# Transposing a gating matrix once, during the first attention layer, instead of in each gating layer

## The chip, the cores and the metric

The kernel runs on one core of a Trainium2 chip, in one launch. The time is that of the device for one execution, in microseconds; five executions were timed, and one more was profiled. The engines are TensorE (PE, matmuls and transposes; PEld is its weight loading), VectorE (DVE), ScalarE (ACT), GpSimd (POOL) and SyncE (SP, which here issues all the transfers).

## The reference

The input x has 2048 rows of 512 numbers in bf16. Four layers follow one another, each added to x: attention, gating, attention, gating. Both attention layers have the same weights, and so have both gating layers.

```python
def _A_ref(x, wq, wk, wv, wo):          # 32 heads of 16, one shared k and v
    q = (x @ wq).reshape(B, S, H, Dh).transpose(0, 2, 1, 3)
    k = x @ wk
    v = x @ wv
    p = softmax(einsum('bhqd,bkd->bhqk', q, k) * Dh ** -0.5)
    o = einsum('bhqk,bkd->bhqd', p, v)
    return o.transpose(0, 2, 1, 3).reshape(B, S, H * Dh) @ wo

def _B_ref(x, w_in, w_sp, b_sp, w_out): # F = 1792, Fh = 896
    z = gelu(einsum('bsd,df->bsf', x, w_in))
    z1 = z[..., :Fh]
    z2 = layernorm(z[..., Fh:])
    g = einsum('ts,bsf->btf', w_sp, z2) + b_sp[None, :, None]
    return einsum('bsf,fd->bsd', z1 * g, w_out)

x = x + _A_ref(layernorm(x), ...)
x = x + _B_ref(layernorm(x), ...)
x = x + _A_ref(layernorm(x), ...)
x = x + _B_ref(layernorm(x), ...)
```

w_sp is a matrix of 2048 x 2048 that mixes rows of x. TensorE sums over the partition dimension, so the product with w_sp needs w_sp with its columns (s) in the partitions: its transpose.

## The kernel before

Every engine has one program, a list of operations in the order in which the Python code calls `K.op`; each operation waits for semaphore values and may raise a semaphore. So the order of the code is the order on each engine. Tiles have 128 partitions; x stays in SBUF as X for the whole kernel.

**Attention (`layer_A`).** After a layer norm (`layer_norm_T`: statistics, normalising, transposing by TensorE) come k, v and two of the 32 projections of q. Then a loop over i runs 683 times. The work is counted in blocks of 128 keys x 512 queries for one head; four heads make a unit (qc, hg, kt), of which there are 4 x 8 x 16 = 512. An iteration handles three blocks:

- `emit_exp(i)` (L585): ScalarE takes the exponential of three PSUM banks of scores at once, 128 x 1536.
- `emit_pv(u)` and `emit_acc(u)` (L600, L618, L620, L622) for a unit whose four blocks are done: TensorE multiplies with v, and VectorE adds the result to an accumulator. Unit u is done in iteration (4u+3)//3, so three of four iterations have a unit. L622 is the last unit of a group of 16, of which there are 32.
- `emit_fill(i + 2)` (L566): TensorE computes the three score blocks of the iteration after the next.
- One side task: `emit_side_pe` and `emit_side_dve` take the next of `side_queue`. The queue begins with the 30 remaining projections of q (L397, L402). Each finished group adds a final task, which transposes and divides by the softmax sum (L479, L484, L489); the last group of a query chunk adds two tasks that transpose (L511, L519) and four that multiply with wo and add to X (L529, L534). All side tasks share PSUM bank 7. What is in the queue when the loop ends is emitted behind it.

**Gating (`layer_B`).** After a layer norm, 60 items (32 of z2, 28 of z1) go through a software pipeline of five steps: matmuls (L695 or L700), square on ScalarE (L732), a multiply on VectorE (L741), tanh on ScalarE (L752), and a last multiply on VectorE (L762), for z2 with statistics (L767, L770). Each item uses one of six slots (PSUM bank, `ybuf`, `thbuf`); matmuls of item k wait for L762 of item k - 6. The five steps are emitted with lags of 0 to 4 items. ScalarE then normalises z2 (L795).

The second half goes through four blocks of 512 rows (tc). For each block, SP loads four times 128 rows of w_sp (L824, 512 KB) into `wsp_stage`, which has two slots; TensorE transposes them in groups of eight 128 x 128 pieces (L839), and VectorE copies each group from PSUM to `wspT` (L847). Then come 7 x 16 matmuls with `wspT` (L868), VectorE's add and multiply (L875, L881), four times seven matmuls with w_out (L897), and the add to X (L903). At the end SP stores X in 16 transfers (L918).

Of the kernel before, what the change touches and what calls it, by code (L numbers as in the profile page):

```python
# [6 lines left out]
BF16 = mybir.dt.bfloat16  # L7
# [97 lines left out]
def bass_interleave_layers__grouped_kv_mqa__mixer_gmlp__prompt_kernel(  # L105
# [13 lines left out]
    S = A_x.shape[1]  # L119
    assert A_x.shape[2] == D  # L120
    assert S % 128 == 0
    NT = S // 128
# [4 lines left out]
    TCW = QC  # L127
# [7 lines left out]
    S_wA = K.sem()  # L135
    S_wB = K.sem()
    S_wsp = [K.sem(), K.sem()]
    S_dpool = K.sem()
    S_pool = K.sem()
    S_ploc = K.sem()  # L140
# [19 lines left out]
    def bank16(b):  # L160
        return ps16[:, 1024 * b:1024 * (b + 1)]
# [77 lines left out]
        w_prep = (S_dve, w_prep_v)  # L239

    x_ready = [(S_x, S_x.n)]
    G = {"stage_free": [None, None]}

    def layer_norm_T(lst, x_waits, extra_pe_waits):
        xnT = K.sb([P, KD, S], BF16, lst, name="xnT")
# [51 lines left out]
        xst.__exit__(None, None, None)  # L297
        return xn, xnT, xnT_v

    def layer_A(layer_idx, x_waits):  # L300
        lst = ExitStack()
        lst.__enter__()
        xn, xnT, xnT_v = layer_norm_T(lst, x_waits, extra_pe_waits=[])
        xnT_all = (S_dve, max(xnT_v))
        qT_pad = K.sb([P, 8, S], BF16, lst, name="qT_pad")
# [121 lines left out]
            return (4 * u + 3) // 3  # L427

        side_queue = []
        side_state = {"k_pe": 0, "k_dve": 0}  # L430
        fin_pe_val = [None, None]
        x_done_vals = []

        def emit_side_pe():
            if side_state["k_pe"] >= len(side_queue):
                return False
            k = side_state["k_pe"]
            task = side_queue[k]
            if task.get("pe_ready") is not None and not task["pe_ready"]():
                return False  # L440
            wl = list(task["pe_waits"]) + [(S_sdve, sdve_base + k)]
            v = K.op("pe", task["pe"], waits=wl, inc=S_spe)
            task["pe_val"] = v
            if "on_pe_emitted" in task:
                task["on_pe_emitted"](v)
            side_state["k_pe"] += 1
            return True

        def emit_side_dve():
            if side_state["k_dve"] >= side_state["k_pe"]:  # L450
                return False
            k = side_state["k_dve"]
            task = side_queue[k]
            wl = list(task["dve_waits"]) + [(S_spe, task["pe_val"])]
            fns = task["dve"]
            v = None
            for idx, fn in enumerate(fns):
                wlx = wl if idx == 0 else [(S_dloc, v)]
                if idx < len(fns) - 1:
                    v = K.op("dve", fn, waits=wlx, inc=S_dloc)  # L460
                else:
                    v = K.op("dve", fn, waits=wlx, inc=S_sdve)
            task["dve_val"] = v
            if "on_dve_emitted" in task:
                task["on_dve_emitted"](v)
            side_state["k_dve"] += 1
            return True
# [3 lines left out]
        pv_bank = bank32(6)  # L471
        for (qc, hg) in q_groups[NQ_PRO:]:
            side_queue.append(make_q_task(qc, hg))

        def make_fin_task(qc, hg, par, acc_val):
            def pe_fn(e):
# [163 lines left out]
        for i in range(NI):  # L640
            emit_exp(i)
            for u in pending_pv.get(i, []):
                emit_pv(u)
                emit_acc(u)
            if i + 2 < NI:
                emit_fill(i + 2)
            emit_side_pe()
            emit_side_dve()
        for i in range(NI, NI + 8):
            for u in pending_pv.get(i, []):  # L650
                emit_pv(u)
# [1 line left out]
        while side_state["k_dve"] < len(side_queue) or side_state["k_pe"] < len(side_queue):  # L653
            progressed = emit_side_pe()
            progressed = emit_side_dve() or progressed
            if not progressed:
                break
        assert side_state["k_dve"] == len(side_queue)
        lst.__exit__(None, None, None)
        return [(S_sdve, max(x_done_vals))]  # L660

    def layer_B(layer_idx, x_waits):
        lst = ExitStack()
# [2 lines left out]
        xnT_all = (S_dve, max(xnT_v))  # L666
        z2n = K.sb([P, NT, FH], BF16, lst, name="z2n")
        z1c = K.sb([P, NF1, S], BF16, lst, name="z1c")
        NSLOT = 6
        ybuf = K.sb([P, NSLOT, 512], FP32, lst, name="ybuf")  # L670
        thbuf = K.sb([P, NSLOT, 512], BF16, lst, name="thbuf")
        st2 = K.sb([P, NT, 2, 6], FP32, lst, name="st2")
# [41 lines left out]
        def step_pe(k):  # L714
            it = items[k]
            slot = k % NSLOT
            bk = bank32(slot)
            wl = [xnT_all, wB]
            if k >= NSLOT:
                wl.append((S_dve, st["d4"][k - NSLOT]))  # L720
            st["pe"][k] = K.op("pe", lambda e, it=it, bk=bk: pe_item(e, it, bk), waits=wl, inc=S_pe)

        def step_a0(k):
            it = items[k]
            slot = k % NSLOT
            bk = bank32(slot)
            n = item_N(it)
            wl = [(S_pe, st["pe"][k])]
            if k >= NSLOT:
                wl.append((S_dve, st["d3"][k - NSLOT]))  # L730
                wl.append((S_act, st["a1"][k - NSLOT]))
            st["a0"][k] = K.op("act", lambda e, slot=slot, bk=bk, n=n: e.activation(  # L732
                ybuf[:, slot, 0:n], bk[:, 0:n], ACTF.Square, scale=SQA), waits=wl, inc=S_act)
# [38 lines left out]
        LAG = [0, 1, 2, 3, 4]  # L772
        for it_k in range(NIT + 5):
            k = it_k
            if k - LAG[0] < NIT and k - LAG[0] >= 0:
                step_pe(k - LAG[0])
            if 0 <= k - LAG[1] < NIT:
                step_a0(k - LAG[1])
            if 0 <= k - LAG[2] < NIT:
                step_d3(k - LAG[2])  # L780
            if 0 <= k - LAG[3] < NIT:
                step_a1(k - LAG[3])
            if 0 <= k - LAG[4] < NIT:
                step_d4(k - LAG[4])
        gelu_done = (S_dve, st["d4"][NIT - 1])
        z1_ready = gelu_done

# [9 lines left out]
                            waits=[(S_dve, vnb), gelu_done], inc=S_act)  # L797
        z2n_all = (S_act, vz2n[NT - 1])

        wsp_stage = K.sb([P, 2, S], BF16, lst, name="wsp_stage")  # L800
        wspT = K.sb([P, NT, TCW], BF16, lst, name="wspT")
        hT2 = K.sb([P, NF1, TCW], BF16, lst, name="hT2")
        gtmp = K.sb([P, 3, TCW], FP32, lst, name="gtmp")

# [2 lines left out]
        wt_bank_free = [None, None]  # L807
        g_bank_free = [None, None, None]
        y_bank_free = [None, None]
        wspT_free = None  # L810
        hT2_free = None
        x_vals = []
        gi_ctr = [0]
        ngrp = 8 if NT >= 8 else NT

        for tc in range(NTC):
            wspT_v = None
            for tt in range(NTT):
                trow = tc * NTT + tt
                slot = tt % 2  # L820
                wl = list(x_waits)
                if stage_free[slot] is not None:
                    wl.append((S_pe, stage_free[slot]))
                vdma_v = K.op("sp", lambda e, slot=slot, trow=trow: e.dma_start(  # L824
                    wsp_stage[:, slot, :], B_w_sp[trow * 128:(trow + 1) * 128, :]), waits=wl, inc=S_wsp[slot], incv=16)
                vdma = (S_wsp[slot], vdma_v)
                for g0 in range(0, NT, ngrp):
                    gsz = min(ngrp, NT - g0)
                    b = gi_ctr[0] % 2
                    bk = bank16(b)  # L830
                    wl = [vdma, (S_pool, v_ident), gelu_done]
                    if wt_bank_free[b] is not None:
                        wl.append((S_dve, wt_bank_free[b]))

                    def pe_tr(e, slot=slot, g0=g0, gsz=gsz, bk=bk):
                        ins = None
                        for k in range(gsz):
                            sti = g0 + k
                            ins = e.transpose(bk[:, k * 128:(k + 1) * 128], wsp_stage[:, slot, sti * 128:(sti + 1) * 128], ident[:])  # L839
                        return ins  # L840
                    vtr = K.op("pe", pe_tr, waits=wl, inc=S_pe)
                    stage_free[slot] = vtr

                    def dve_cp(e, g0=g0, gsz=gsz, tt=tt, bk=bk):
                        dst = wspT[:, g0:g0 + gsz, tt * 128:(tt + 1) * 128]
                        src = bk[:, 0:gsz * 128].rearrange("p (k q) -> p k q", q=128)
                        return e.tensor_copy(dst, src)  # L847
                    wlc = [(S_pe, vtr)]
                    if g0 == 0 and tt == 0 and wspT_free is not None:
                        wlc.append((S_pe, wspT_free))  # L850
                    vcp = K.op("dve", dve_cp, waits=wlc, inc=S_dve)
                    wt_bank_free[b] = vcp
                    wspT_v = vcp
                    gi_ctr[0] += 1
            wspT_ready = (S_dve, wspT_v)

            vh = [None] * NF1
            for ft in range(NF1):
# [3 lines left out]
                if g_bank_free[gb] is not None:  # L862
                    wl.append((S_dve, g_bank_free[gb]))

                def pe_g(e, ft=ft, bk=bk):
                    ins = None
                    for sti in range(NT):
                        ins = e.matmul(bk[:, 0:TCW], z2n[:, sti, ft * 128:(ft + 1) * 128], wspT[:, sti, :],  # L868
                                       start=(sti == 0), stop=(sti == NT - 1))
                    return ins  # L870
                vg = K.op("pe", pe_g, waits=wl, inc=S_pe)
                if ft == NF1 - 1:
                    wspT_free = vg
                wl = [(S_pe, vg), v_bsp_w]
                v1 = K.op("dve", lambda e, gb=gb, bk=bk, tc=tc: e.tensor_tensor(  # L875
                    gtmp[:, gb, :], bk[:, 0:TCW], bsp_bc[:, tc * TCW:(tc + 1) * TCW], ALU.add),
# [31 lines left out]
        return [(S_dve, max(x_vals))]  # L908

    xw = x_ready  # L910
    xw = layer_A(0, xw)
    xw = layer_B(1, xw)
    xw = layer_A(2, xw)
    xw = layer_B(3, xw)
# [2 lines left out]
    for t in range(NT):  # L917
        v = K.op("sp", lambda e, t=t: e.dma_start(out[0, t * 128:(t + 1) * 128, :], X[:, t, :]),  # L918
                 waits=list(xw), inc=S_out, incv=16)
    K.op("sp", lambda e: e.nop(nofuse=True), waits=[(S_out, v)])  # L920
    K.op("pool", lambda e: e.nop(nofuse=True), waits=[(S_out, v)])
    K.emit()


# [26 lines left out]
```

## Time and profile before

| what | value |
|---|---|
| median of five runs | 2753.64 us (2751.88 to 2755.23) |
| profiled execution | 2760.63 us, its span 2758.8 us |
| busy share of the span | PE 72%, PEld 20%, DVE 45%, ACT 76%, POOL 0% |
| mean granted TensorE clock | 0.627 of full speed |
| first attention layer, from its layer norm | about 23 to 1082 us of the span |
| first gating layer | about 1082 to 1387 us |
| second attention layer | about 1387 to 2447 us |
| second gating layer | about 2447 to 2756 us |

The granted clock is that of TensorE as a share of 2.4 GHz; 0.50 is 1.2 GHz. A busy time counts the instructions of an engine, and in a row of the timeline the bracket says how long the engine was idle before it and which instruction ended that. A matmul's duration in the trace includes the time until its result is written, so that one instruction's time can overlap the next one's.

### The profile page before, as it was taken

How to read it: one execution, taken by the hardware profiler on the slowest of the kernel's cores; microseconds unless marked ns; L12 is line 12 of the kernel's file. 1: busy time of each engine (PE TensorE's matmuls, PEld its weight loads, DVE VectorE, ACT ScalarE, POOL GpSimd, SP SyncE). 2: the span in 40 equal slices, each digit the busy share in tenths (PEclk: the TensorE clock that was granted, in tenths of full speed). 3: DMA queues.
4: the chain of work that ended last, by engine and by line, in shares of the span. 5: the costliest groups of instructions: out<-in, count | busy, mean ns of one | idle time of the engine just before them, and what ended most of it. 6: DMA issues, size and time to landing. Idle time of an engine off the chain costs nothing.

```text
span 2758.8 us, 30002 instructions
## 1 busy us (share of the span) xinstructions
PE 1982.4 (72%) x11488; PEld 565.5 (20%) x11488; DVE 1243.1 (45%) x2067; ACT 2092.5 (76%) x1653; POOL 0.7 (0%) x7
## 2 busy tenths in 40 slices
PE   3877777777776775678967777777777777756787
PEld 2211111111111111234422111111111111121343
DVE  5533433343333335954365334333433433369433
ACT  1899999999999994560038999999999999936400
POOL 0000000000000000000000000000000000000000
PEclk9855555555555555888987555555555555559889
DMA  2000000000000000001000000000000000000121
GB/s 94 1 1 1 1 1 1 1 1 1 1 0 1 1 1 16 1 31 61 16 1 1 0 1 1 1 1 1 1 1 1 1 1 1 1 16 0 32 61 46
DMA packets 12812, 27.25 MB, mean 10 GB/s; under 512 B 1920, under 2 KB 7936, under 8 KB 12672
## 3 DMA queue, kind: packets, MB, share of 16 engines
q1 hardware_dynamic: 12672, 25.33, 2.9%
q8 instruction: 94, 1.54, 0.2%
q14 instruction: 46, 0.38, 0.0%
HBM read 23.23 MB, written 2.10 MB: 9 GB/s over the span
## 4 chain that ended last, share of the span: by engine, by line
PE 45%; DVE 29%; ACT 19%; issue 5%; DMA 1%; SPq 0%; ACTq 0%
PE ps_all L600 21%; ACT P_ring L585 17%; DVE acc_sb L620 14%; PE ps_all L868 8%; PE ps_all L566 7%; PE ps_all L397 2%; DVE ybuf L741 2%; PE ps_all L897 2%; PE ps_all L529 2%; DVE st L767 1%; DVE qT_pad L402 1%; DVE ln_stats L251 1%; DVE z2n L762 1%; ACT z2n L795 1%; DVE oT_bf L622 1%
## 5 line engine op out<-in xcount | busy, mean ns | idle before, releaser
L585 ACT ACTIVATE P_ring<-ps_all 128x1536 bf16<-128x1536 f32 (+1 forms) x1366 | 1918.3, 1449 | 141.7 <-PE ps_all L566 107.4
L620 DVE TENSOR_TENSOR acc_sb<-ps_all,acc_sb 128x512 f32<-128x512 f32 x896 | 619.2, 691 | 1001.4 <-PE ps_all L600 1001.2
L600 PE MATMUL ps_all<-P_ring,V_aug 128*32 128x512 bf16 x4096 | 614.6, 587 | 487.9 <-ACT P_ring L585 277.6
L566 PE MATMUL ps_all<-qT_pad,kT_rep 32*128 32x512 bf16 x4096 | 802.6, 584 | 19.3 <-ACT P_ring L585 5.0
L600 PEld LDWEIGHTS ps_all<-P_ring,V_aug 128*32 128x32 bf16 x4096 | 130.4, 100 | 969.8 <-ACT P_ring L585 931.0
L566 PEld LDWEIGHTS ps_all<-qT_pad,kT_rep 32*128 32x128 bf16 x4096 | 141.9, 98 | 602.0 <-issue 440.6
L868 PE MATMUL ps_all<-wspT,z2n 128*128 128x512 bf16 x896 | 213.1, 404 | 19.3 <-ACT z2n L795 14.5
L258 ACT ACTIVATE ln_veps<-ln_mv,eps_c 128x16 f32<-128x16 f32 x4 | 1.2, 308 | 265.3 <-DVE ln_mv L255 265.3
L868 PEld LDWEIGHTS ps_all<-wspT,z2n 128*128 128x128 bf16 x896 | 91.6, 103 | 138.8 <-issue 24.2
L752 ACT ACTIVATE thbuf<-ybuf 128x448 bf16<-128x448 f32 (+1 forms) x120 | 72.2, 602 | 54.3 <-DVE ybuf L741 50.6
L875 DVE TENSOR_TENSOR gtmp<-ps_all,bsp_bc 128x512 f32<-128x512 f32 x56 | 38.7, 692 | 158.8 <-PE ps_all L868 158.8
L695 PE MATMUL ps_all<-w_in_r,xnT 128*128 128x448 bf16 x256 | 64.9, 387 | 42.0 <-DVE z2n L762 40.1
L280 PE MATMUL ps_all<-ident,xn 128*128 128x128 bf16 x256 | 27.3, 292 | 87.4 <-DVE xn L264 73.7
L732 ACT ACTIVATE ybuf<-ps_all 128x448 f32<-128x448 f32 (+1 forms) x120 | 66.5, 554 | 27.9 <-PE ps_all L695 27.5
L622 DVE TENSOR_TENSOR oT_bf<-ps_all,acc_sb 128x512 bf16<-128x512 f32 x64 | 44.3, 692 | 74.5 <-PE ps_all L600 74.5
L741 DVE SCALAR_TENSOR_TENSOR ybuf<-ybuf,ps_all 128x448 f32<-128x448 f32 (+1 forms) x120 | 75.6, 630 | 3.7 <-ACT ybuf L732 3.2
L839 PE MATMUL ps_all<-ident,wsp_stage 128*128 128x128 bf16 x512 | 48.8, 270 | 35.6 <-DMA wsp_stage<-in_B_w_sp_dram 21.2
L397 PE MATMUL ps_all<-xnT,wq_pad 128*128 128x512 bf16 x240 | 64.3, 392 | 12.1 <-DVE qT_pad L402 6.5
L700 PE MATMUL ps_all<-xnT,w_in_r 128*128 128x512 bf16 x224 | 61.2, 400 | 13.9 <-DVE z1c L762 8.7
L402 DVE CAST qT_pad<-ps_all 128x512 bf16<-128x512 f32 x60 | 41.5, 692 | 48.8 <-PE ps_all L397 48.8
L897 PE MATMUL ps_all<-w_out_r,hT 128*128 128x512 bf16 x224 | 49.7, 379 | 12.1 <-DVE hT L881 12.1
L847 DVE COPY wspT<-ps_all 128x1024 bf16<-128x1024 bf16 x64 | 43.0, 689 | 30.6 <-PE ps_all L839 30.4
(62 smaller groups left out, 776.3 us busy)
## 6 DMA issues: line engine op xcount, KB each, us to landing
wsp_stage<-in_B_w_sp_dram SPq DMA_DIRECT2D x32, 512.0 KB, 3.6
X<-in_A_x_dram SPq DMA_DIRECT2D x1, 2048.0 KB, 8.6
out_dram<-X SPq DMA_DIRECT2D x16, 128.0 KB, 1.8
w_in_r<-in_B_w_in_dram SPq DMA_DIRECT2D x1, 1792.0 KB, 9.5
w_out_r<-in_B_w_out_dram SPq DMA_DIRECT2D x1, 896.0 KB, 10.7
wq_nat<-in_A_wq_dram SPq DMA_DIRECT2D x1, 512.0 KB, 9.7
wo_r<-in_A_wo_dram SPq DMA_DIRECT2D x1, 512.0 KB, 6.4
bsp_bc<-in_B_b_sp_dram SPq DMA_DIRECT2D x1, 512.0 KB, 10.8
```

Source lines behind the costliest of these rows:

```text
L397: ins = e.matmul(side_bank32[:, 0:QC], wq_pad[:, kd, hg, :], xnT[:, kd, qc * QC:(qc + 1) * QC], start=(kd == 0), stop=(kd == KD - 1))
L402: return e.tensor_copy(qT_pad[:, hg, qc * QC:(qc + 1) * QC], side_bank32[:, 0:QC])
L566: ins = e.matmul(bk[:, 0:QC], kT_rep[32 * j:32 * j + 32, kt * 128:(kt + 1) * 128], qT_pad[32 * j:32 * j + 32, hg, qc * QC:(qc + 1) * QC], ...
L585: return e.activation(P_ring[:, s0:s0 + n, :], bank32(b0, n).rearrange("p (k q) -> p k q", k=n)[:, :, 0:QC], ACTF.Exp, scale=DH ** -0.5)
L600: ins = e.matmul(pv_bank[32 * j:32 * j + 32, 0:QC], V_aug[:, kt, 32 * j:32 * j + 32], P_ring[:, slot, :], tile_position=(0, 32 * j), start ...
L620: fn = lambda e: e.tensor_tensor(acc_sb[:], pv_bank[:, 0:QC], acc_sb[:], ALU.add)
L622: fn = lambda e: e.tensor_tensor(oT_bf[:, par, :], pv_bank[:, 0:QC], acc_sb[:], ALU.add)
L732: st["a0"][k] = K.op("act", lambda e, slot=slot, bk=bk, n=n: e.activation(ybuf[:, slot, 0:n], bk[:, 0:n], ACTF.Square, scale=SQA), waits=w ...
L741: st["d3"][k] = K.op("dve", lambda e, slot=slot, bk=bk, n=n: e.scalar_tensor_tensor(ybuf[:, slot, 0:n], ybuf[:, slot, 0:n], GELU_C, bk[:, ...
L752: st["a1"][k] = K.op("act", lambda e, slot=slot, n=n: e.activation(thbuf[:, slot, 0:n], ybuf[:, slot, 0:n], ACTF.Tanh), waits=wl, inc=S_act)
L868: ins = e.matmul(bk[:, 0:TCW], z2n[:, sti, ft * 128:(ft + 1) * 128], wspT[:, sti, :], start=(sti == 0), stop=(sti == NT - 1))
L897: ins = e.matmul(bk[:, 0:D], hT2[:, ft, tt * 128:(tt + 1) * 128], w_out_r[:, ft, :], start=(ft == 0), stop=(ft == NF1 - 1))
```

## The change

Both gating layers use the same w_sp. The changed kernel transposes it once, in the first attention layer, and keeps the transpose in device memory:

- The first attention layer gets 32 more side tasks (`make_wspt_task`, in `late_queue`): eight transposes on TensorE into bank 7 and one copy by VectorE each. Rows are staged by SP (`emit_stage_dma`, two slots), and two tasks fill a tile of 128 rows, which SP stores to `wspT_d` in device memory (2048 pieces of 256 bytes). The tile has two slots too; VectorE waits for the store of two tiles ago. A late task enters the side queue only when that is empty.
- In both attention layers, once the 30 projections of q are issued, a side task is emitted only in iterations with i % 4 == 3 (and behind the loop).
- The gating layers lose the staging, the transposes and the copies. For each block SP loads 2 MB of the transpose into one of two `wspT` buffers.
- The GELU pipeline has four slots instead of six, and its five steps are emitted in the reverse order, the oldest item first.

```diff
-    def layer_A(layer_idx, x_waits):
+    def layer_A(layer_idx, x_waits, do_wspt=False):
...
+        if do_wspt:
+            wsp_stage2 = K.sb([P, 2, S], BF16, lst, name="wsp_stage2")
+            wspT_tile = K.sb([P, 2, NT, 128], BF16, lst, name="wspT_tile")
...
+        n_q = len(side_queue)
...
+            def emit_stage_dma(tt):
+                slot = tt % 2
+                wl = [w_prep]
+                if tt >= 2:
+                    wl.append((S_spe, wst["pe2_val"][tt - 2]))
+                v = K.op("sp", lambda e, slot=slot, tt=tt: e.dma_start(
+                    wsp_stage2[:, slot, :], B_w_sp[tt * 128:(tt + 1) * 128, :]), waits=wl, inc=S_wsp[slot], incv=16)
+                wst["dma_val"][tt] = (S_wsp[slot], v)
+
+            def make_wspt_task(tt, h):
...
+                def pe_fn(e):
+                    ins = None
+                    for k in range(nst):
+                        sti = 8 * h + k
+                        ins = e.transpose(side_bank16[:, k * 128:(k + 1) * 128],
+                                          wsp_stage2[:, slot, sti * 128:(sti + 1) * 128], ident[:])
+                    return ins
+
+                def dve_fn(e):
+                    dst = wspT_tile[:, tslot, 8 * h:8 * h + nst, :]
+                    src_ = side_bank16[:, 0:nst * 128].rearrange("p (k q) -> p k q", q=128)
+                    return e.tensor_copy(dst, src_)
...
+                if h == 0 and tt >= 2:
+                    task["dve_waits_fn"] = lambda tslot=tslot: [(S_wt[tslot], wst["tile_dma_val"][tslot])]
+                if h == NH - 1:
+                    def on_pe(v, tt=tt):
+                        wst["pe2_val"][tt] = v
+                        if tt + 2 < NT:
+                            emit_stage_dma(tt + 2)
+                    task["on_pe_emitted"] = on_pe
+
+                    def on_dve(v, tt=tt, tslot=tslot):
+                        vd = K.op("sp", lambda e, tslot=tslot, tt=tt: e.dma_start(
+                            wspT_dv[:, :, tt * 128:(tt + 1) * 128], wspT_tile[:, tslot, :, :]),
+                            waits=[(S_sdve, v)], inc=S_wt[tslot], incv=16)
...
+            for tt in range(NT):
+                for h in range(NH):
+                    late_queue.append(make_wspt_task(tt, h))
...
-            emit_side_pe()
-            emit_side_dve()
+            if late_queue and i % 4 == 3 and side_state["k_pe"] == len(side_queue):
+                side_queue.append(late_queue.pop(0))
+            if side_state["k_pe"] < n_q or i % 4 == 3:
+                emit_side_pe()
+                emit_side_dve()
...
-        NSLOT = 6
+        NSLOT = 4
...
+            if 0 <= k - LAG[4] < NIT:
+                step_d4(k - LAG[4])
+            if 0 <= k - LAG[3] < NIT:
+                step_a1(k - LAG[3])
+            if 0 <= k - LAG[2] < NIT:
+                step_d3(k - LAG[2])
+            if 0 <= k - LAG[1] < NIT:
+                step_a0(k - LAG[1])
             if k - LAG[0] < NIT and k - LAG[0] >= 0:
                 step_pe(k - LAG[0])
...
-        wsp_stage = K.sb([P, 2, S], BF16, lst, name="wsp_stage")
-        wspT = K.sb([P, NT, TCW], BF16, lst, name="wspT")
+        wspT = K.sb([P, 2, NT, TCW], BF16, lst, name="wspT")
...
+            wb = tc % 2
+            wl = list(x_waits) + list(G["wspt_done"])
+            if wspT_free[wb] is not None:
+                wl.append((S_pe, wspT_free[wb]))
+            vld = K.op("sp", lambda e, wb=wb, tc=tc: e.dma_start(wspT[:, wb, :, :], wspT_dv[:, :, tc * TCW:(tc + 1) * TCW]),
+                       waits=wl, inc=S_wsp[wb], incv=16)
+            wspT_ready = (S_wsp[wb], vld)
```

The lines of L816 to L855 that stage, transpose and copy are gone.

## Rows read from the trace of the kernel before

**Rows 1.** The page: granted TensorE clock in 40 equal slices, in tenths.

```profile
PEclk9855555555555555888987555555555555559889
```

**Rows 2.** The chain of waits, first gating layer: start us, us, engine, what.

```profile
1201.81 16.51 ACT z2n L795 x16
...
1262.53 27.14 PE ps_all L868 x112
```

**Rows 3.** Six stretches, L897 to next L868: PE, PEld, DVE, ACT, POOL; clock, DMA, GB/s.

```profile
1252.95:1262.53 9.58, 5.55 (x66) 4.63 (x64) 5.94 (x9) 0.00 (x0) 0.00 (x0) 0.76 0.52 164
...
sum 58.70, PE 34.01 PEld 28.60 DVE 35.66 ACT 0.00 POOL 0.00; mean PE 5.67 PEld 4.77 DVE 5.94 ACT 0.00 POOL 0.00
```

**Rows 4.** Stretches of the six L868 blocks that follow those gaps.

```profile
2716.49:2740.85 24.36, 24.35 (x112) 10.89 (x112) 8.30 (x12) 0.00 (x0) 0.00 (x0) 1.00 0.00 0
sum 159.21, PE 159.10 PEld 68.52 DVE 49.82 ACT 0.00 POOL 0.00; mean PE 26.52 PEld 11.42 DVE 8.30 ACT 0.00 POOL 0.00
```

**Rows 5.** A stretch: the first microseconds of an L868 block.

```profile
1262.50:1266.00 3.50, 3.47 (x9) 1.27 (x10) 0.00 (x0) 0.00 (x0) 0.00 (x0) 0.50 0.57 154
```

**Rows 6.** Timeline of ScalarE, first attention layer (idle before, in brackets).

```profile
319.42 2.96 ACT L585 ACTIVATE P_ring<-ps_all 128x1536 bf16<-128x1536 f32 x2 [0.50 <-PE ps_all L566]
...
415.25 61.38 ACT L585 ACTIVATE P_ring<-ps_all 128x1536 bf16<-128x1536 f32 x43 [0.50 <-PE ps_all L566]
477.14 30.14 ACT L585 ACTIVATE P_ring<-ps_all 128x1536 bf16<-128x1536 f32 x21 [0.51 <-PE ps_all L566]
```

**Rows 7.** L585's idle time (us, times), 120 to 1080 us and 1484 to 2430 us.

```profile
PE ps_all L566: 19.1, 33
...
PE ps_all L566: 19.7, 35
```

**Rows 8.** Timeline of all engines around three side tasks, first attention layer.

```profile
251.15 7.23 ACT L585 ACTIVATE P_ring<-ps_all 128x1536 bf16<-128x1536 f32 x5
...
254.87 0.61 PE L566 MATMUL ps_all<-qT_pad,kT_rep 32*128 32x512 bf16 x3
...
256.27 0.61 PE L566 MATMUL ps_all<-qT_pad,kT_rep 32*128 32x512 bf16 x3
...
318.76 0.61 PE L566 MATMUL ps_all<-qT_pad,kT_rep 32*128 32x512 bf16 x3
...
319.31 1.03 PE L511 MATMUL ps_all<-ident,o_norm 128*128 128x128 bf16 x8
...
323.18 1.89 PE L529 MATMUL ps_all<-wo_r,onT 128*128 128x512 bf16 x4
```

**Rows 9.** Timeline of all engines, GELU pipeline, z1 items.

```profile
1177.38 0.68 DVE L762 SCALAR_TENSOR_TENSOR z1c<-thbuf,ps_all 128x512 bf16<-128x512 bf16 x1
1177.50 0.63 ACT L752 ACTIVATE thbuf<-ybuf 128x512 bf16<-128x512 f32 x1
1177.98 0.68 DVE L741 SCALAR_TENSOR_TENSOR ybuf<-ybuf,ps_all 128x512 f32<-128x512 f32 x1
1178.03 0.58 ACT L732 ACTIVATE ybuf<-ps_all 128x512 f32<-128x512 f32 x1
...
1178.12 1.04 PE L700 MATMUL ps_all<-xnT,w_in_r 128*128 128x512 bf16 x4 [0.16 <-DVE z1c L762]
1178.58 0.68 DVE L762 SCALAR_TENSOR_TENSOR z1c<-thbuf,ps_all 128x512 bf16<-128x512 bf16 x1
```

**Rows 10.** Transfers: KB each and median us to landing; the output's issue on SP.

```profile
wsp_stage<-in_B_w_sp_dram SPq DMA_DIRECT2D x32, 512.0 KB, 3.6
X<-in_A_x_dram SPq DMA_DIRECT2D x1, 2048.0 KB, 8.6
out_dram<-X SPq DMA_DIRECT2D x16, 128.0 KB, 1.8
...
2749.32 7.72 SPq L918 DMA_DIRECT2D out_dram<-X  x16
```

**Rows 11.** The page, costliest groups: one of VectorE.

```profile
L847 DVE COPY wspT<-ps_all 128x1024 bf16<-128x1024 bf16 x64 | 43.0, 689 | 30.6 <-PE ps_all L839 30.4
```

More of the change, by code (lines that the diff above doesn't have):

```diff
@@ L137, in bass_interleave_layers__grouped_kv_mqa__mixer_gmlp__prompt_kernel @@
     S_wsp = [K.sem(), K.sem()]
+    S_wt = [K.sem(), K.sem()]
     S_dpool = K.sem()
@@ L241, in bass_interleave_layers__grouped_kv_mqa__mixer_gmlp__prompt_kernel @@
     x_ready = [(S_x, S_x.n)]
-    G = {"stage_free": [None, None]}
+    G = {"stage_free": [None, None], "wspt_done": None}
+    wspT_d = nc.dram_tensor("wspt_scratch", [NT, P, S], BF16)
+    wspT_dv = wspT_d.ap().rearrange("st p t -> p st t")
     def layer_norm_T(lst, x_waits, extra_pe_waits):
@@ L429, in layer_A @@
         side_queue = []
+        late_queue = []
         side_state = {"k_pe": 0, "k_dve": 0}
@@ L441, in emit_side_pe @@
             wl = list(task["pe_waits"]) + [(S_sdve, sdve_base + k)]
+            if "pe_waits_fn" in task:
+                wl += list(task["pe_waits_fn"]())
             v = K.op("pe", task["pe"], waits=wl, inc=S_spe)
@@ L454, in emit_side_dve @@
             wl = list(task["dve_waits"]) + [(S_spe, task["pe_val"])]
+            if "dve_waits_fn" in task:
+                wl += list(task["dve_waits_fn"]())
             fns = task["dve"]
@@ L473, in layer_A @@
             side_queue.append(make_q_task(qc, hg))
+        n_q = len(side_queue)
+        if do_wspt:
+            wst = {"dma_val": [None] * NT, "tile_dma_val": [None, None], "pe2_val": [None] * NT}
+            NH = (NT + 7) // 8
+            def emit_stage_dma(tt):
[7 more added lines that the diff above has]
+            def make_wspt_task(tt, h):
+                slot = tt % 2
+                tslot = tt % 2
+                nst = min(8, NT - 8 * h)
+                def pe_fn(e):
[9 more added lines that the diff above has]
+                    return e.tensor_copy(dst, src_)
+                task = {"pe": pe_fn, "pe_waits": [(S_pool, v_ident)], "dve": [dve_fn], "dve_waits": [],
+                        "pe_waits_fn": (lambda tt=tt: [wst["dma_val"][tt]])}
+                if h == 0 and tt >= 2:
[10 more added lines that the diff above has]
+                            waits=[(S_sdve, v)], inc=S_wt[tslot], incv=16)
+                        wst["tile_dma_val"][tslot] = vd
+                        if tt == NT - 1:
+                            G["wspt_done"] = [(S_wt[0], S_wt[0].n), (S_wt[1], S_wt[1].n)]
+                    task["on_dve_emitted"] = on_dve
+                return task
+            emit_stage_dma(0)
+            if NT > 1:
+                emit_stage_dma(1)
+            for tt in range(NT):
+                for h in range(NH):
+                    late_queue.append(make_wspt_task(tt, h))
@@ L657, in layer_A @@
                 break
-        assert side_state["k_dve"] == len(side_queue)
+        assert side_state["k_dve"] == len(side_queue) and not late_queue
         lst.__exit__(None, None, None)
-        return [(S_sdve, max(x_done_vals))]
+        ret = [(S_sdve, max(x_done_vals))]
+        if do_wspt:
+            ret += list(G["wspt_done"])
+        return ret
     def layer_B(layer_idx, x_waits):
@@ L719, in step_pe @@
             if k >= NSLOT:
+                assert st["d4"][k - NSLOT] is not None
                 wl.append((S_dve, st["d4"][k - NSLOT]))
@@ L774, in layer_B @@
             k = it_k
+            if 0 <= k - LAG[4] < NIT:
[6 more added lines that the diff above has]
+                step_a0(k - LAG[1])
             if k - LAG[0] < NIT and k - LAG[0] >= 0:
                 step_pe(k - LAG[0])
[L777 to L784, printed above, removed]
         gelu_done = (S_dve, st["d4"][NIT - 1])
@@ L809, in layer_B @@
         y_bank_free = [None, None]
-        wspT_free = None
+        wspT_free = [None, None]
         hT2_free = None
@@ L816, in layer_B @@
         for tc in range(NTC):
[L817 to L854, printed above, removed]
@@ L855, in layer_B @@
-            wspT_ready = (S_dve, wspT_v)
+            wb = tc % 2
[5 more added lines that the diff above has]
+            wspT_ready = (S_wsp[wb], vld)
             vh = [None] * NF1
@@ L863, in layer_B, with pe_g @@
                     wl.append((S_dve, g_bank_free[gb]))
-                def pe_g(e, ft=ft, bk=bk):
+                def pe_g(e, ft=ft, bk=bk, wb=wb):
                     ins = None
                     for sti in range(NT):
-                        ins = e.matmul(bk[:, 0:TCW], z2n[:, sti, ft * 128:(ft + 1) * 128], wspT[:, sti, :],
+                        ins = e.matmul(bk[:, 0:TCW], z2n[:, sti, ft * 128:(ft + 1) * 128], wspT[:, wb, sti, :],
                                        start=(sti == 0), stop=(sti == NT - 1))
@@ L872, in layer_B @@
                 if ft == NF1 - 1:
-                    wspT_free = vg
+                    wspT_free[wb] = vg
                 wl = [(S_pe, vg), v_bsp_w]
@@ L910, in bass_interleave_layers__grouped_kv_mqa__mixer_gmlp__prompt_kernel @@
     xw = x_ready
-    xw = layer_A(0, xw)
+    xw = layer_A(0, xw, do_wspt=True)
     xw = layer_B(1, xw)
@@ L919, in bass_interleave_layers__grouped_kv_mqa__mixer_gmlp__prompt_kernel @@
                  waits=list(xw), inc=S_out, incv=16)
-    K.op("sp", lambda e: e.nop(nofuse=True), waits=[(S_out, v)])
-    K.op("pool", lambda e: e.nop(nofuse=True), waits=[(S_out, v)])
+    fin_w = [(S_out, v)] + list(G["wspt_done"])
+    K.op("sp", lambda e: e.nop(nofuse=True), waits=fin_w)
+    K.op("pool", lambda e: e.nop(nofuse=True), waits=fin_w)
     K.emit()
```

## The prediction

> **What bounds the kernel now.** I read the slices of the page first: the granted clock of TensorE is about half in the two long attention stretches and 0.8 to 0.9 in the gating layers [rows 1], so the layers have different limits and each is read from its own rows.
>
> In a gating layer the chain of waits runs through TensorE. ScalarE normalises z2 for 16.5 us, and then block after block of L868 takes some 27 us [rows 2]. Between the last matmul of L897 and the first of the next L868 lie six gaps (three in each layer, none before the first block), in which the transposes of L839 wait for a staging transfer, two buffers deep: from 9.16 to 10.29 us, together 58.70 [rows 3]. What the gap does afterwards stands in the next view: the blocks that follow one begin at a granted clock of 0.50, the lower level of 1.2 GHz [rows 5], and take 26.7 to 27.1 us; one happens to start at 1.00 (2.4 GHz) and takes 24.36. The six sum to 159.21 [rows 4].
>
> In attention, ScalarE's exponentials run back to back (30.14/21 = 1.435 us each) for 20 to 43 at a time, and then pause 0.50 us, and at the end of a query chunk several times in a row [rows 6]. Past the projection of q the pauses sum to 19.1 us in 33 and 19.7 in 35 [rows 7]; twenty in each layer are the single 0.50 kind, 10.1 us, so 9.0 and 9.6 belong to the three chunk ends. These pauses are where the side tasks (L479, L511, L529) stand in TensorE's order; ScalarE's total is the layer's time, so a pause removed or added counts in full.
>
> **Removed: transposes from the gating layers.** Block 0's transposes lie under the 16.5 us of z2 [rows 2] and give nothing. The six gaps go: in TensorE's order the next L868 now stands directly behind L897, and its PSUM banks and operands are older. That is -58.7 us [rows 3]. With no gap the clock has no reason to fall between L897 and L868; five blocks go from their time to that of the one that started at 1.00: 159.21 - 6 x 24.36 = 13.05, so -13.1 us [rows 4, 5]. If the clock fell all the same, this term would be 0. The first block of each layer follows the 16.5 us pause as before and stays slow.
>
> **Added: loading the transposed matrix.** Four transfers of 2 MB in each gating layer, in rows of 1 KB, the shape of the X load that took 8.6 us [rows 10]. The first two are issued at the layer's start, some 100 us ahead of use. The third waits for block 0's last matmul and is needed after L897, block 1 and L897 again, over 24 us of matmul alone [rows 4]; the fourth likewise. SP's queue holds nothing else then. Cost 0; without that cover it would be some 8.6 us a transfer, as a gap.
>
> **Added: 32 transpose tasks in the first attention layer; moved: every side task, in both.** After the q tasks, a side task is issued only in each fourth iteration. The unit index (4u+3)//3 puts no PV product in the iteration that follows (i % 4 = 0), so the task stands between two score fills. The room there can be read at 254.87: the fill occupies TensorE 0.55 us (318.76 to 319.31), so a task can start at 255.42; the next fill's exponential starts 0.66 us after the fill (318.76 to 319.42); the exponentials from 251.15 are due at 251.15 + 4 x 1.435 = 256.89; so the fill may begin as late as 256.23. Room: 0.81 us [rows 6, 8]. A final task (L479) that the old order happened to place there pushed the fill to 256.27, and the five exponentials took 7.23 us instead of 7.17, with no pause: about free [rows 8].
> - Final tasks: the 40 single pauses of 0.505 us vanish, -20.2 us [rows 6, 7]. Cost bounds of what is left: 0 to 0.06 each.
> - New tasks: eight transposes, as L511, 1.03 us with the drain, 0.96 without it (the fill's 0.61 against 0.55 shows the drain), so 0.15 over the room: 32 x 0.15 = +4.8 [rows 8]. Bounds: 0 (room enough) and 0.96 each (no room), 31 us. I take 0.15, since the final task in this very place cost no more than 0.06. Their copies on VectorE fall before the next accumulation is ready.
> - L511 tasks: 12 in slots (six a layer; those of the last chunk stay behind the loop), 12 x 0.15 = +1.8. L529 tasks: 24, 1.89 less the same drain = 1.82, 1.01 over the room: +24.2 [rows 8]. The burst at the chunk end before raised its own clock; spread out, I expect the low level. At the high level a set of four takes 1.04 [rows 9], about 0.2 over the room, 5 us in all; with no room 44. Against these 26.0 stand the 18.6 us of chunk-end pauses that go [rows 7]: net +7.4.
>
> **Added: staging and scratch transfers on SP's queue.** A new task's load (512 KB, 3.6 us, [rows 10]) is issued three slots ahead, 3 x 4 x 1.435 = 17.2 us. The store of a transposed row block has the same three slots less VectorE's copy of 0.69 [rows 11], 16.5 us, before VectorE waits for its buffer, with the accumulations, then PV, then ScalarE behind it. The trace has no store in 256-byte pieces. The nearest rows: 16 output stores, also 2048 pieces, were issued within 7.72 us and one lands in 1.8, so 9.5 at most; from below, 3.6 for the same bytes inward; from above 16 x 1.8 = 28.8, if nothing overlapped [rows 10]. I take at most 9.5, as its count of pieces is the same, hence hidden: 0. The Trainium skill, page "DMA: Bandwidth & Descriptors", section "Specifications", says a transfer below 512 bytes makes the engine read before it writes; no run here shows that. If it doubled the 9.5, an estimate, the store would take 19.0 us and the sum would lose 17 us by the working of the third rival.
>
> **Changed: four slots for the GELU pipeline, issued in reverse.** VectorE sets its pace: in the z1 items L762 starts each 1.20 us, TensorE waiting 0.16 us for it [rows 9]. The tightest new loop covers three items: L762 0.68, matmuls 1.04, square 0.58, tanh 0.63, four handovers of 0.06 (L762's end to the matmul): 3.2/3 = 1.06 us, below 1.20 [rows 9]. The loop over four items adds L741's 0.68: 3.9/4 = 0.98. At the low clock (1.89 for the matmuls) the first becomes 4.0/3 = 1.35. z2 items carry statistics on VectorE besides and have more slack. I take 0; bounds 0 and 0.15 x 56 = 8 us.
>
> **Sum.** -58.7 - 13.1 - 20.2 + 7.4 + 4.8 = -79.8 us. The profiled execution took 2760.6 (span 2758.8); it would take 2680.8. The shown runs have a median of 2753.6, 7 us less, so 2673.8.
>
> **Rivals.**
> 1. The clock still falls in front of L868: the half-rate start remains, 2673.8 + 13.1 = 2686.9. For it: each of the first blocks, and five of the six that followed a gap, start low; against it: those starts come after pauses with waits, and the remaining wait between L868 and L897 is short.
> 2. There is no room in the slots, and each task costs ScalarE its whole time: 32 x 0.96 + 12 x 0.96 + 24 x 1.82 = 85.9 instead of 18.6 + 20.2, so +47.1 instead of -8.0: 2728.9. Against it: the free final task [rows 8].
> 3. The scratch store is slow. At w us each second row block waits w - 16.5, seven times in all (its neighbour is shifted along with it). At 19.0 that is 17 us: 2691. It eats the whole gain at 16.5 + 79.8/7 = 27.9 us; at the upper bound 28.8 it costs 86 and ends at 2760, slower. Only a store of pieces wholly one after the other does that; the output's issue rate speaks against it [rows 10].
> 4. Added tasks raise the clock in attention, as the burst did: L529 and the new tasks fit nearly, some 20 us less: 2654.
> 5. Four slots bind at the low clock: at most 8 us, 2682.
>
> **How the numbers follow.** The forecast has 0.60, rival 1 0.10, rival 2 0.08, rival 3 0.06 (0.04 of it near 2691, 0.02 slower), rival 4 0.08, rival 5 0.06, something unseen 0.02. The range reaches from rival 4 to past rivals 1 and 5 and the milder third, 2654 to 2696. About 0.2%, 5 us, is what a measurement tells from no change. Slower by more: 0.03; within it: 0.02; faster: 0.95.
>
> **What would show it.** Right: L868 directly behind L897 with no idle time but loading, the later blocks at 24.4 us and clock 1.00; exponentials in unbroken chains across the final tasks; pauses of about 1 us at L529 and of 0.1 to 0.2 at the new tasks; z1 items still 1.20 us apart. Wrong: VectorE waiting for the scratch store, L868 waiting for its load, pauses near 1 us at each new task, or TensorE waiting in the GELU stage for L762 with VectorE idle.

## The result and the profile after

The changed kernel takes 2662.4 us (2661.2 to 2663.8, 8 runs); the runs of the kernel before on the same chips have a median of 2755.2. The ratio is 0.9665, with a 95% interval of 0.9655 to 0.9674: 92.9 us less. The forecast was 2673.8, in a range of 2654 to 2696, from a change of -79.8. Direction and range hold; the gain is 13 us larger than worked out. The two profiled executions differ by 96.8 us of span (2758.8 and 2662.0), and the rest of the comparison is of those two.

The chain of waits names the start of each layer norm, so it gives the layers. First the kernel before, then the changed kernel (start us, us, what):

```profile
23.01 8.98 DVE ln_stats L251 x15
...
1082.23 9.60 DVE ln_stats L251 x16
...
1386.97 9.61 DVE ln_stats L251 x16
...
2447.59 9.61 DVE ln_stats L251 x16
```

```profile
22.72 8.99 DVE ln_stats L254 x15
...
1069.83 9.61 DVE ln_stats L254 x16
...
1206.45 27.01 PE ps_all L913 x112
1234.96 6.22 PE ps_all L942 x28
1241.18 24.19 PE ps_all L913 x112
...
1337.64 9.60 DVE ln_stats L254 x16
...
2385.98 9.60 DVE ln_stats L254 x16
```

Subtracting the starts gives a table; the second gating layer runs to the end of the span. The forecast by layer uses the prediction's terms where they arise: each attention layer -10.1 for its final tasks, -9.0 or -9.6 for its chunk-end pauses and half of 26.0 for the tasks in slots, the first also +4.8; each gating layer its three gaps of [rows 3] and its share of [rows 4].

| layer | before | after | difference | forecast |
|---|---|---|---|---|
| attention 1 | 1059.2 | 1047.1 | -12.1 | -1.3 |
| gating 1 | 304.7 | 267.8 | -36.9 | -37.4 |
| attention 2 | 1060.6 | 1048.3 | -12.3 | -6.7 |
| gating 2 | 311.2 | 276.0 | -35.2 | -34.4 |

The gating layers came out as worked out; the attention layers gained 16 us more. In the fence, L942 (the old L897) ends at 1241.18 and L913 (the old L868) starts at 1241.18: the gap of [rows 3] is gone. The blocks behind it, by stretch (PE, PEld, DVE, ACT, POOL, clock, DMA share, GB/s):

```profile
1241.18:1265.37 24.19, 24.18 (x113) 10.78 (x110) 9.00 (x13) 0.00 (x0) 0.00 (x0) 1.00 0.00 0
...
sum 145.14, PE 145.05 PEld 64.66 DVE 53.97 ACT 0.00 POOL 0.00; mean PE 24.17 PEld 10.78 DVE 9.00 ACT 0.00 POOL 0.00
```

All six run at a granted clock of 1.00 from their first matmul; 145.14 stands against the 159.21 of [rows 4]. Only the first block of a layer is still slow (27.01 and 26.27).

ScalarE's timeline in the first attention layer, where L656 is the old L585, answers to [rows 6]:

```profile
114.42 220.23 ACT L656 ACTIVATE P_ring<-ps_all 128x1536 bf16<-128x1536 f32 x154 [0.37 <-PE ps_all L637]
335.56 5.67 ACT L656 ACTIVATE P_ring<-ps_all 128x1536 bf16<-128x1536 f32 x4 [0.91 <-PE ps_all L637]
342.13 5.67 ACT L656 ACTIVATE P_ring<-ps_all 128x1536 bf16<-128x1536 f32 x4 [0.91 <-PE ps_all L637]
348.59 5.48 ACT L656 ACTIVATE P_ring<-ps_all 128x1536 bf16<-128x1536 f32 x4 [0.78 <-PE ps_all L637]
354.79 228.65 ACT L656 ACTIVATE P_ring<-ps_all 128x1536 bf16<-128x1536 f32 x160 [0.72 <-PE ps_all L637]
```

The reader is to see three things. The 0.50 us pauses at the final tasks are gone. The first chain, 154 long, runs over 28 of the 32 new tasks (the last ends at 389) without a pause; idle bits of about 0.06 us, of which more at the end, are too short for the timeline to show. The four pauses that are left stand at the L529 tasks (now L600); in the two layers all pauses sum to 8.7 us in 12 and 8.5 in 11, where [rows 7] had 19.1 and 19.7. Also, the fours that follow a pause are short: 5.67 and 5.48 us. At 1.435 us an exponential, as the prediction had it, four could not take less than 3 x 1.435 + 1.45 = 5.76. That is where the working was wrong, and the experiments go after it.

### The profile page after: what moved, and what is told of

Read it like the earlier page. It is cut to its first block, busy times and chain, and to the rows that moved or that the text cites. A ratio compares the mean times of both kernels' runs of the same rounds, so it can differ in the third digit from the quotient of the medians.

```text
span 2662.0 us, 29476 instructions
## 1 busy us (share of the span) xinstructions
PE 1964.1 (74%) x11232; PEld 547.1 (21%) x11232; DVE 1229.2 (46%) x2035; ACT 2090.4 (79%) x1653; POOL 0.7 (0%) x7
## 3 DMA queue, kind: packets, MB, share of 16 engines
q8 instruction: 92, 1.51, 0.2%
## 4 chain that ended last, share of the span: by engine, by line
PE 47%; DVE 27%; ACT 20%; issue 5%; DMA 0%; SPq 0%; ACTq 0%
PE ps_all L671 21%; ACT P_ring L656 19%; DVE acc_sb L691 13%; PE ps_all L637 8%; PE ps_all L913 7%; PE ps_all L403 2%; DVE ybuf L819 2%; PE ps_all L600 2%; PE ps_all L942 2%; DVE st L845 2%; DVE qT_pad L408 2%; DVE ln_stats L254 1%; DVE z2n L840 1%; ACT z2n L873 1%; DVE z1c L840 1%
## 5 line engine op out<-in xcount | busy, mean ns | idle before, releaser
L656 ACT ACTIVATE P_ring<-ps_all 128x1536 bf16<-128x1536 f32 (+1 forms) x1366 | 1916.1, 1449 | 119.5 <-PE ps_all L637 84.9
L913 PE MATMUL ps_all<-wspT,z2n 128*128 128x512 bf16 x896 | 199.3, 385 | 42.5 <-ACT z2n L873 42.5
L913 PEld LDWEIGHTS ps_all<-wspT,z2n 128*128 128x128 bf16 x896 | 88.8, 99 | 152.1 <-ACT z2n L873 43.5
L689 DVE COPY acc_sb<-ps_all 128x512 f32<-128x512 f32 x64 | 44.2, 691 | 43.7 <-PE ps_all L671 43.7
L600 PE MATMUL ps_all<-wo_r,onT 128*128 128x512 bf16 x128 | 57.9, 605 | 6.3 <-DVE X L605 4.7
L942 PE MATMUL ps_all<-w_out_r,hT 128*128 128x512 bf16 x224 | 49.7, 379 | 12.1 <-DVE hT L926 12.1
```

The source lines that it names most:

```text
L600: ins = e.matmul(side_bank32[:, 0:D], onT[:, par, c, qt * 128:(qt + 1) * 128], wo_r[:, c, :], start=(c == 0), stop=(c == 3))
L656: return e.activation(P_ring[:, s0:s0 + n, :], bank32(b0, n).rearrange("p (k q) -> p k q", k=n)[:, :, 0:QC], ACTF.Exp, scale=DH ** -0.5)
L942: ins = e.matmul(bk[:, 0:D], hT2[:, ft, tt * 128:(tt + 1) * 128], w_out_r[:, ft, :], start=(ft == 0), stop=(ft == NF1 - 1))
```

## The experiments

Each differs from one of the two kernels by the edit shown; ratios are to the kernel before. Theory S is the prediction's: ScalarE is saturated in attention, so whatever delays an exponential counts in full. Theory L was formed from the fours. It says that attention waits for a loop over all engines, which can be followed in the steady state of the kernel before:

```profile
245.58 0.62 PE L600 MATMUL ps_all<-P_ring,V_aug 128*32 128x512 bf16 x4 [0.89 <-ACT P_ring L585]
...
246.25 0.69 DVE L620 TENSOR_TENSOR acc_sb<-ps_all,acc_sb 128x512 f32<-128x512 f32 x1 [2.02 <-PE ps_all L600]
...
247.09 0.62 PE L600 MATMUL ps_all<-P_ring,V_aug 128*32 128x512 bf16 x4 [0.35 <-DVE acc_sb L620]
...
248.60 0.62 PE L600 MATMUL ps_all<-P_ring,V_aug 128*32 128x512 bf16 x4 [0.34 <-DVE acc_sb L620]
...
249.15 1.26 PE L566 MATMUL ps_all<-qT_pad,kT_rep 32*128 32x512 bf16 x6
...
251.31 0.62 PE L600 MATMUL ps_all<-P_ring,V_aug 128*32 128x512 bf16 x4 [0.90 <-ACT P_ring L585]
```

There is one PSUM bank for the product with v, so product and accumulation alternate: 1.51 us each from 245.58 to 247.09 and to 248.60. Behind the third product stands the fill (0.55 later); its exponential starts 0.66 after it ([rows 6, 8]) and takes 1.45; then comes the next product: 1.51 + 1.51 + 0.55 + 0.66 + 1.45 + 0.06 = 5.74 us, and the trace has 251.31 - 245.58 = 5.73 for four exponentials. ScalarE itself could do four in 4 x (5.48 - 1.45)/3 = 5.37.

**The spacing of the side tasks alone.** The kernel before, with this edit only:

```diff
-            emit_side_pe()
-            emit_side_dve()
+            if side_state["k_pe"] < n_q or i % 4 == 3:
+                emit_side_pe()
+                emit_side_dve()
```

Expected: 

> The kernel before, with nothing changed but that side tasks behind the projections of q are emitted in each fourth iteration. Theory S, that of the prediction (ScalarE is saturated in attention, 1.435 us an exponential, and 0.81 us fit into a slot): final tasks -20.2, L511 and L529 tasks +7.4, so -12.8 us against before. Theory L (what sets attention's pace is the loop product with v, accumulation, product, accumulation, product, score fill, exponential; 0.98 us fit into a slot): -12.3 in each layer, as the second attention layer of the changed kernel shows, -24.7 us.

Measured: 2730.0 us against 2755.2, ratio 0.9913 (0.9894 to 0.9932): -25.2. That is twice the number of S, which lies outside the interval. It is also L's number, but that one had been read off the second attention layer of the changed kernel, not worked out from the loop; so this run shows what the spacing alone is worth, and the loop itself is put to the test by the fill further down. Its ScalarE timeline has a chain of the same 154 exponentials, here with no new tasks among them:

```profile
115.32 220.12 ACT L586 ACTIVATE P_ring<-ps_all 128x1536 bf16<-128x1536 f32 x154 [0.37 <-PE ps_all L567]
```

220.12 against 220.23 in the changed kernel: the 28 new tasks in that stretch cost 0.1 us together.

**The spacing undone.** The changed kernel, with that condition taken out again.

```diff
-            if side_state["k_pe"] < n_q or i % 4 == 3:
-                emit_side_pe()
-                emit_side_dve()
+            emit_side_pe()
+            emit_side_dve()
```

Expected: 

> The changed kernel, but the old side tasks are emitted in every iteration again; the new transposes still enter only in each fourth, when the queue is empty. Theory S: the spacing was worth 12.8 us, so +12.8 against the changed kernel, 2675. Theory L: it was worth some 24 us, so 2686, with the 0.50 us pauses back.

Measured: 2687.5, ratio to before 0.9758 (0.9743 to 0.9772), 25.2 us more than the changed kernel. The pauses are back:

```profile
225.74 61.58 ACT L656 ACTIVATE P_ring<-ps_all 128x1536 bf16<-128x1536 f32 x43 [0.50 <-PE ps_all L637]
```

So the change has two parts that add up: the spacing, -25.2, and the rest, -67.7. The spacing needs no transposed matrix at all.

**Four slots alone.** The kernel before with four GELU slots and, not shown in the cut, its five steps in the reversed order.

```diff
-        NSLOT = 6
+        NSLOT = 4
```

Expected: 

> The kernel before with four slots for the GELU pipeline and the reversed order of its steps, and nothing else. The prediction: VectorE's 1.20 us an item is longer than any new loop, so no difference (within 2 us). The rival, four slots bind at the low clock: up to +8 us.

Measured: 2756.9, ratio 1.0007 (0.9997 to 1.0018): no difference. In the changed kernel's trace the z1 items stand as in [rows 9], 1.20 us apart, TensorE waiting 0.16 us:

```profile
1161.89 0.68 DVE L840 SCALAR_TENSOR_TENSOR z1c<-thbuf,ps_all 128x512 bf16<-128x512 bf16 x1
...
1162.63 1.04 PE L777 MATMUL ps_all<-xnT,w_in_r 128*128 128x512 bf16 x4 [0.16 <-DVE z1c L840]
1163.09 0.68 DVE L840 SCALAR_TENSOR_TENSOR z1c<-thbuf,ps_all 128x512 bf16<-128x512 bf16 x1
```

**The fill first.** The changed kernel, with the score fill ahead of the product in TensorE's order, which takes the accumulations out of the loop:

```diff
+            if i + 2 < NI:
+                emit_fill(i + 2)
             for u in pending_pv.get(i, []):
                 emit_pv(u)
                 emit_acc(u)
-            if i + 2 < NI:
-                emit_fill(i + 2)
```

Expected: 

> The changed kernel, but in each iteration of attention the score fill stands ahead of the product with v in TensorE's order. Theory S: ScalarE is saturated at 1.435 us an exponential, so the order on TensorE changes nothing: 2662, or a few us more from the side tasks. Theory L: the fill, and so the exponential, no longer waits for the accumulations; ScalarE then repeats in 1.343 us (the pace of the unbroken fours of 5.48 us), 0.087 us less for 651 exponentials in each of two layers, -113 us; the room in a slot becomes 0.86 us of a shorter period, +14 for the side tasks: about 2563.

Measured: 2582.9, ratio to before 0.938 (0.9366 to 0.9394), 79.5 us less than the changed kernel, with the same work. S, which gives nothing here, has fallen. L overshot by 20 us, and the trace shows on what: at some final tasks, which now wait for a later accumulation, a pause of 0.67 us, which the expectation had left out; at most new tasks 0.15 in front of a four of 5.48, so 0.26 more than 5.37; at most L529 tasks 1.01. The granted clock stayed where it was (0.51 from 118 to 330 us, 0.50 in the changed kernel).

```profile
145.55 5.48 ACT L656 ACTIVATE P_ring<-ps_all 128x1536 bf16<-128x1536 f32 x4 [0.15 <-PE ps_all L637]
...
433.75 86.08 ACT L656 ACTIVATE P_ring<-ps_all 128x1536 bf16<-128x1536 f32 x64 [0.67 <-PE ps_all L637]
```

**The fill first, and another slot.** As before, with side tasks where i % 4 == 0.

```diff
-            if late_queue and i % 4 == 3 and side_state["k_pe"] == len(side_queue):
+            if late_queue and i % 4 == 0 and side_state["k_pe"] == len(side_queue):
...
-            if side_state["k_pe"] < n_q or i % 4 == 3:
+            if side_state["k_pe"] < n_q or i % 4 == 0:
```

Expected: 

> The changed kernel with the score fill ahead of the product with v, and the side tasks emitted where i % 4 == 0, behind a fill with no product after it. Theory L: as with the fill first, ScalarE at 1.343 us, and a slot has room for 1.41 us, so only L529 is over, by 0.41 us: -113 and a few us less for the side tasks, about 2546. Theory S: no gain, 2662, or some us more or less from the other slot.

Measured: 2551.7, ratio to before 0.9258 (0.9244 to 0.9272), 110.7 us less than the changed kernel. This version beats both kernels. Its timeline in the steady state:

```profile
399.35 14.06 ACT L656 ACTIVATE P_ring<-ps_all 128x1536 bf16<-128x1536 f32 x10
...
401.37 0.61 PE L637 MATMUL ps_all<-qT_pad,kT_rep 32*128 32x512 bf16 x3 [0.19 <-ACT P_ring L656]
...
401.99 0.62 PE L671 MATMUL ps_all<-P_ring,V_aug 128*32 128x512 bf16 x4
...
405.40 0.61 PE L637 MATMUL ps_all<-qT_pad,kT_rep 32*128 32x512 bf16 x3 [0.74 <-ACT P_ring L656]
...
410.77 0.61 PE L637 MATMUL ps_all<-qT_pad,kT_rep 32*128 32x512 bf16 x3 [0.74 <-ACT P_ring L656]
```

Now TensorE waits for ScalarE in front of a fill, and four exponentials take 410.77 - 405.40 = 5.37 us: this is what a saturated ScalarE looks like here.

**Longer new tasks.** The changed kernel with the first four transposes of each new task done twice.

```diff
-                    for k in range(nst):
+                    for k in list(range(4)) + list(range(nst)):
```

Expected: 

> The changed kernel with twelve transposes instead of eight in each new task (the first four done twice, the result is the same): 1.44 us of TensorE instead of 0.96. Theory S (room 0.81): each costs 0.63, 20.2 us in all, where eight cost 4.8. Theory L (room 0.98): 0.46 each, 14.7, where eight cost nothing. Against the changed kernel, which has no pause at the new tasks, S leaves 15 to 20 and L 15 us: 2677 either way or up to 2682; the layer's own time tells more: under L some 14.7 us above the second attention layer without new tasks, under S 20.

Measured: 2670.4, ratio 0.9686 (0.9667 to 0.9705), 8 us more than the changed kernel; S had asked for 15 to 20, L for 15, so both missed the total. Where the clock is low the price is L's:

```profile
176.79 5.67 ACT L656 ACTIVATE P_ring<-ps_all 128x1536 bf16<-128x1536 f32 x4 [0.48 <-PE ps_all L637]
182.95 5.67 ACT L656 ACTIVATE P_ring<-ps_all 128x1536 bf16<-128x1536 f32 x4 [0.48 <-PE ps_all L637]
```

A pause of 0.48 and a short four: 6.16 us instead of 5.73, so 0.43 a task (L had 0.46, S 0.63). So it is at 27 of the 32 tasks, with a pause of 0.42 to 0.48 at a granted clock of 0.50; 27 x 0.43 = 11.6 us, and the first attention layer is 9.2 us longer than in the changed kernel. The other five have no pause: during four of them the clock was up (0.61, 0.68, and 1.00 twice), and at the fifth it had just been up. From 118 to 330 us it was 0.58, where the changed kernel had 0.50. That the clock made the difference was not tried by itself.

**One buffer for the loaded transpose.** The load of a block waits for the last matmul of the block before.

```diff
-            wb = tc % 2
+            wb = 0
```

Expected: 

> The changed kernel with one buffer for the loaded transpose instead of two, so that a block's load is issued when the last matmul of the block before is done. Cover is then the wait for VectorE and L942, 1.5 + 6.1 = 7.6 us, against 8.0 us to landing plus the issue: a gap of about 0.5 to 1 us before three blocks in each layer, +3 to +6 us, the clock staying high. If loads need more than their landing time shows, or disturb L942, more than 10 us.

Measured: 2668.0, ratio 0.9682 (0.9667 to 0.9697), 5.7 us more than the changed kernel. L942 and the wait ahead of it, 7.72 us, hide all but 0.3 to 0.6 us of five of the loads and all but 1.5 of the sixth, and blocks take 24.36 us each in the chain instead of 24.19.

**A gap without work.** As that one, but the load waits for L942 too.

```diff
                 if tt == NTT - 1:
                     hT2_free = vy
+                    wspT_free[wb] = vy
```

Expected: 

> As the one with one buffer, but the load is issued only when L942 is done: TensorE then idles for the load, about 8.2 us, six times, with no transposes in the gap: +49 us. If the gap itself brings the clock down, the blocks behind it take some 26.8 us instead of 24.2 and the sum is +65, 2727; if in the kernel before it was the transposes in the gap, or chance, that left the clock low, the blocks stay at 24.2 and it is +49, 2711.

Measured: 2724.6, ratio 0.9885 (0.987 to 0.9901), 62.3 us more than the changed kernel, near the 65 of the falling clock. Its chain of waits shows a gap and the block behind it, and the stretches below it the clock:

```profile
1240.78 7.85 DMA wspT<-wspt_scratch
1248.68 25.87 PE ps_all L913 x112
```

```profile
1248.68:1252.00 3.32, 3.32 (x9) 1.27 (x10) 0.00 (x0) 0.00 (x0) 0.00 (x0) 0.54 0.02 5
1252.00:1274.00 22.00, 22.00 (x104) 9.97 (x103) 8.30 (x12) 0.00 (x0) 0.00 (x0) 1.00 0.00 0
```

TensorE does nothing in the gap and starts behind it at a granted clock of 0.54, and at 0.50 behind the five others. The six blocks sum to 158.9 us, 13.8 more than the 145.1 without a gap: the idle time alone brings the clock down, and it costs what the prediction put on it. Gaps in which TensorE transposes, as in the kernel before, do so less surely: one of the six blocks behind them started at 1.00 there, and in the profile of the four slots alone three of the six did, at 24.36 us each. The six sum to 153.9 us there, so the clock cost 7.7 us in that execution, not 13.1.

## Why the prediction was right, and where its size was off

- **Gaps removed, -58.7.** Right: L913 follows L942 at once in all three places of each layer. Together with the clock, the two gating layers lost 72.1 us against 71.8.
- **Clock kept, -13.1.** Right: 145.14 us for six blocks where 146.2 was expected. The run with an empty gap shows the mechanism. That the size fits is in part luck: it is that of one execution of the kernel before, and another had 7.7.
- **Loads hidden, 0.** Right: two megabytes landed in 8.0 us (7.8 to 13.5), with tens of microseconds to spare. With the cover cut to L942 it still cost only 5.7 us for six loads.
- **Staging and scratch, 0.** Right: a store of 2048 pieces landed in 5.0 us (3.8 to 5.2), against a cover of 16.5 and a bound of 9.5. The third rival falls with it. The Trainium skill, page "DMA: Bandwidth & Descriptors", section "Specifications", has such short transfers read before they write. No run shows whether this one does; its 5.0 us are less than double the 3.9 that the same bytes inward took.
- **Four slots, 0.** Right, by the run that changes them alone.
- **Final tasks, -20.2.** Right about the pauses and about in size: the single pauses are gone, and two chains with their pauses took 61.38 + 0.50 + 30.14 + 0.51 = 92.5 us [rows 6], where the unbroken chain, at 1.43 an exponential, needs 91.5 for 64.
- **New tasks, +4.8: mis-sized.** The 28 compared above cost 0.1 us together, and the forecast took 0.15 a task.
- **L511 and L529 tasks, +7.4: mis-sized, in sign too.** The forecast put 26.0 us of new cost against 18.6 of pauses that go. The pauses in their place sum to 17.2, and behind each, the short fours give some of it back: from 335.56 to 342.13 four exponentials and the pause take 6.57 us, 0.84 more than 5.73, and from 348.59 to 354.79, after the clock had risen, 0.47, where 1.01 was put on each. By difference (-24.4 in both attention layers, less -20.2 and 0.1) these tasks came to -4.3 us.

The step that failed is "ScalarE's total is the layer's time, so a pause removed or added counts in full", and with it the room of 0.81 us in a slot, which took the exponentials as due each 1.435 us. The unbroken chains of ScalarE were paced by the loop through product and accumulation. ScalarE had 5.73 - 5.37 = 0.36 us to spare in four, so a fill that came 0.15 us late delayed one exponential and nothing else. What must not be late is the product behind that fill. It waits for the exponential that ends at 256.89 (by the prediction's working), plus 0.06, and the fill ahead of it takes 0.55, so the fill may start at 256.40 and not only at 256.23: from 255.42 that is 0.98 us of room [rows 8]; in the trace that product starts at 257.03, which would make it 1.06. The new tasks (0.96, free), the longer ones (1.44 - 0.43 = 1.01 at the low clock) and L529 (1.82 - 0.84 = 0.98) agree with it. That attention waits for the loop is shown by putting the fill first: the same work at the same granted clock takes 79.5 us less, which a ScalarE that sets the pace by itself leaves no room for.

The first rival fell with the blocks at 1.00, the second with the unbroken chain, the fourth with a clock of 0.50 during the new tasks (above it only around L529 tasks: 0.61 from 330 to 360 us), the fifth with the four slots alone. What stays open is how much of the difference between the longer tasks' 8 us and 0.43 us for each of the 32 is due to the clock.

## What to carry to other kernels

An engine whose instructions seem to touch in the timeline need not be the limit: follow the steady state back over the engines for one whole period, and compare its length with the engine's shortest repeat anywhere in the trace. If a period is a loop, look at the order in which an in-order queue holds its links; here an exchange of two places was worth 79.5 us, where the whole change was worth 92.9. Work that must go somewhere goes where that loop is not waiting, and moving the old side tasks there gained more than the new ones cost.

## What the runs showed of the hardware

Exponentials of 128 x 1536 have a median duration of 1.451 us in the trace but can start each 1.34 us, as durations overlap. With the fill first the median reads 1.565 us, and in the last version, where ScalarE is saturated, 1.97, though each starts 1.34 us after the one before. So the starts tell the pace, and the durations do not. How busy ScalarE reads tells little more. The stretches give PE, PEld, DVE, ACT, POOL, clock, DMA share and GB/s, first of the changed kernel, then of the last version:

```profile
118.00:330.00 212.00, 181.22 (x1159) 54.71 (x1156) 102.64 (x156) 208.01 (x149) 0.00 (x0) 0.50 0.28 70
```

```profile
343.00:555.00 212.00, 173.58 (x1030) 37.16 (x1030) 91.67 (x142) 212.00 (x159) 0.00 (x0) 0.51 0.02 6
```

At 5.73 us for four, ScalarE is busy for 208.01 of 212 us, 98%, with about 0.11 us idle in each four; at 5.37 for all of 212. The Trainium skill, page "Perfetto Trace Analysis", section "Identifying the Most-Contended Engine", takes ScalarE's occupancy as a fair measure of how near it is to its limit; in this case 6% were left at an occupancy of 98%, and the measurement decides.
